# A kernel whose instruction order is planned at build time: the plan is refined backwards from the end, and block sums of v move to 32-column groups

## Chip, cores, metric

One core of one Trainium2 chip runs the program. The metric is device microseconds of one execution. PE is the matrix engine (PEld its weight loads), DVE the vector engine, ACT the scalar engine, POOL GpSimd, SP the engine that issues most DMA transfers.

## What is computed

Banded attention with block summaries, then a gated feed-forward layer, then a three-way maximum layer; all in 32-bit floats.

```
q, k, v: [2, 8, 768, 64]                       # batch, heads, sequence, head width
k_sum = max over blocks of 32 keys             # 24 per head
v_sum = mean over blocks of 32 values          # 24 per head
scores = [q k^T within |i-j| < 16,  q k_sum^T + log 32] / 8
x  = softmax(scores) @ [v, v_sum]              # -> [1536, 512]
x1 = (sigmoid(x w_gate) * (x w_val)) w_out     # 512 -> 1536 -> 512
h  = max(x1 w1, x1 w2, x1 w3)                  # 512 -> 768
out = h w_out2                                 # 768 -> 512
```

## The kernel before

The attention is cut into 16 units: a batch, a pair of heads p (4) and a half a of the sequence. Units 1 to 4 are batch 0, first half, head pairs 0 to 3; units 5 to 8 are its second half; units 9 to 16 are batch 1. A unit runs, in this order: scores on PE (L663), maximum with mask on DVE (`maxi`, L670, result `e`), exponential on ACT (`expo`, L676), reciprocal of the sum on DVE (L681, L682), scaling of one half on ACT (`scale`, L690) and, in the first eight units, of the other half on DVE (`norm`, L685), transposition on PE (`turn`, L695), copy to `at` on ACT (L701), product with v on PE (`pv`, L708), and the split of the result into two float parts `x`: the high part on ACT (L362), the low part on DVE (L365). Every operand of a large product is split so, and a product is three matmuls of 384 columns (a group of 6 or 12 in the listings is two or four such products).

The large products follow. L800 are the gate and value projections of batch 0, L839 the output projections, L1032 and L933 products of seven blocks in place of eight (a Strassen scheme) for batch 1 and for the second layer, L1133 the last layer. A projection of L800 needs `x` of head pair p for its quarter kc = p, so the quarter kc = 3 of the second half needs unit 8. L800 cannot start before the transpositions of units 1 to 4 (they use the same four PSUM banks, tag `m`). Weights arrive as 64-bit integers and are rebuilt by three DVE operations (L421, L426, L430), then split by ACT (L362, `w`) and DVE (L365).

Nothing of this order is written out by hand. `add(engine, duration, due, function, deps, new, uses, after)` makes a task; `Plan.order()` lists tasks forwards: at each step it takes, of the tasks that can start first on each engine, the one with the lowest due time, with durations and latencies that stand in the code. The due times are set by formulas of constants at the top of the file (`T - 11`, `due[key] + 2.4`). The order that comes out is the order of the instructions on every engine, and an engine runs its instructions strictly in that order. Where `order()` sees PE idle before the first products it adds matmuls of zeros on a tile `idle` (L1195), so as to keep PE busy.

The mean of the values over blocks of 32 is a product with a constant matrix `avg`, 96 rows by 128 columns, of which only columns 96 to 119 are not zero: v lies with 4 partial rows per partition step, 8 values in the free dimension. For batch 0 `vsum` does 8 matmuls of 128 columns that accumulate in one PSUM tile; `vcopy` (ACT, L595) brings the result to `vs`, and `vfill` (DVE, L654) puts it beside v in `vt`.

Of the kernel before, what the change touches and what calls it, by code (L numbers as in the profile page):

```python
# [37 lines left out]
JOINT = 1  # L38
SWITCH = 6.0
PAD = 2.0  # L40
SLACK = {"PE": 0.05, "DVE": 0.12, "ACT": 0.1, "POOL": 0.0, "SP": 0.0}
OVER = 0.0
SLOW = 1.12
# [31 lines left out]
class Plan:  # L75
# [42 lines left out]
    def order(self):  # L118
        engs = ("PE", "DVE", "ACT", "POOL", "SP")
        free = dict.fromkeys(engs, 0.0)  # L120
        free["SP"] = 0.6
        dge = ring = 0.0
        clock = self.Clock()
        free["PE"] = 1.13
        tab = "E"
        taken = {}
        wait, then, ready = {}, {}, {e: [] for e in engs}
        for t in self.tasks:
            pre = t.deps + t.after
            wait[t] = len(pre)  # L130
            for d in pre:
                then.setdefault(d, []).append(t)
            if not pre:
                ready[t.eng].append(t)
        out = []

        def earliest(t):
            at = free[t.eng]
            for d in t.deps:
                more = t.pad if d.eng != t.eng else 0.0  # L140
                if d.dma and d.end > self.CALM:
                    more = max(more, self.LATE)
                at = max(at, d.end + self.lag(d, t) + more)
            for d in t.after:
                at = max(at, d.start)
            need = {}
            for b in t.new:
                k = need.get(b.tag, 0)
                need[b.tag] = k + 1
                used = taken.setdefault(b.tag, [])  # L150
                i = len(used) + k - b.n
                if i >= 0:
                    for d in used[i].users:
                        if d.end is None:
                            return None
                        at = max(at, d.end + (self.LATE if d.dma and d.end > self.CALM else 0.1 if d.eng != t.eng else 0.0))
            return at

        def pressing(x):
            return x[1].due + (SWITCH if x[1].tab and x[1].tab != tab else 0.0)  # L160

        while len(out) < len(self.tasks):
            best = None
            for e in engs:
                c = [(at, t) for at, t in ((earliest(t), t) for t in ready[e]) if at is not None]
                if not c:
                    continue
                first = min(at for at, _ in c)
                at, t = min((x for x in c if x[0] <= first + SLACK[e]), key=pressing)
                if best is None or at < best[0]:  # L170
                    best = at, t
            at, t = best
            ready[t.eng].remove(t)
            t.start = at
            t.end = at + t.dur
            if t.eng == "PE":
                if t.new and at < FIRST + 5.0:
                    width = min(384, t.new[0].shape[-1] * (t.new[0].shape[1] if len(t.new[0].shape) == 3 else 1))
                    now = free["PE"]
                    while True:  # L180
                        end = clock.run(now, width / 2400.0, 1.0, False)
                        if end > at + OVER:
                            break
                        now = clock.run(now, width / 2400.0, 1.0) + 0.001
                        t.idle += 1
                    at = t.start = max(at, now)
                t.end = clock.run(at, t.dur, t.rows)
            if t.dma:
                dge = max(dge, at) + t.dma
                ring = max(ring, dge + 0.65) + (t.dur * SLOW if t.eng == "SP" else 0.2)  # L190
                free[t.eng] = at + t.dur if t.eng != "SP" else dge + 0.025
                t.end = ring
            if t.tab and t.tab != tab:
                tab = t.tab
                t.end += self.TABLE
            if not t.dma:
                free[t.eng] = t.end
            for b in t.new:
                taken[b.tag].append(b)
            out.append(t)  # L200
            for d in then.get(t, ()):
                wait[d] -= 1
                if not wait[d]:
                    ready[d.eng].append(d)
        return out


@with_exitstack
def kernel(
# [51 lines left out]
    ident = constant("ident", [128, 128])  # L261
    masks = constant("masks", [128, 3, CW])
    avg = constant("avg", [96, 128])

    def build_consts():
        make_identity(nc, ident)

        nc.gpsimd.memset(avg, 0.0)
        a = avg[:, 96:CW]
        nc.gpsimd.memset(a, 1.0 / BLK)  # L270
        nc.gpsimd.affine_select(
            out=a, in_=a, pattern=[[-4, NB]], compare_op=ALU.is_ge, fill=0.0,
            base=0, channel_multiplier=1)
        nc.gpsimd.affine_select(
            out=a, in_=a, pattern=[[4, NB]], compare_op=ALU.is_ge, fill=0.0,
            base=3, channel_multiplier=-1)


        nc.gpsimd.memset(masks[:, :, 0:96], 0.0)
        nc.gpsimd.memset(masks[:, :, 96:CW], math.log(BLK) / SC)  # L280
        for par in range(2):
            m = masks[64 * par:64 * par + 64, :, 0:96]
            nc.gpsimd.affine_select(
                out=m, in_=m, pattern=[[0, 3], [1, 96]], compare_op=ALU.is_ge, fill=BIG,
                base=-1, channel_multiplier=-1)
            nc.gpsimd.affine_select(
                out=m, in_=m, pattern=[[0, 3], [-1, 96]], compare_op=ALU.is_ge, fill=BIG,
                base=2 * WIN - 1, channel_multiplier=1)
        nc.gpsimd.memset(masks[0:64, 0, 0:WIN], BIG)
        nc.gpsimd.memset(masks[64:128, 2, 96 - WIN:96], BIG)  # L290
# [276 lines left out]
    def make_sums(b, p, T):  # L567

        kt, lk = load_task("k", BANKS_K, [128, S + 2 * WIN], kn[b, p], 1.14, T - (KEYS if b else KEYS0))
        r, lr = load_task("vn", 2, [96, 2, 8 * D], vn[b, p], 1.092, T - (SUMS if b else SUMS0))  # L570
        ks = Buf(ap_, [128, NB], F32, "ks", 4)
        vs = Buf(ap_, [128, 2 * D], F32, "vs", 4)
        ps = psum_s([128, 2 * D])

        def kmax():
            nc.vector.tensor_reduce(
                out=ks.t, in_=kt.t[:, WIN:WIN + S].rearrange("p (n w) -> p n w", w=BLK), axis=AX.X, op=ALU.max)

        def vsum():

            for n in range(8):
                nc.tensor.matmul(
                    ps.t, lhsT=avg, rhs=r.t[:, :, D * n:D * n + D], start=(n == 0), stop=(n == 7))

        def vadd():
            for n in (4, 2, 1):
                nc.vector.tensor_tensor(
                    out=r.t[:, :, 0:n * D] if n > 1 else vr.t, in0=r.t[:, :, 0:n * D],
                    in1=r.t[:, :, n * D:2 * n * D], op=ALU.add)

        def vmean():
            nc.tensor.matmul(ps.t, lhsT=avg, rhs=vr.t, start=True, stop=True)

        def vcopy():
            nc.scalar.activation(out=vs.t, in_=ps.t, func=ACTF.Copy)  # L595

        k = add("DVE", 0.87, T - 13.5, kmax, [lk], [ks], [kt])
        if b == 0:
            v1, v2 = None, add("PE", 1.75, T - 5, vsum, [lr, built], [ps], [r])
        else:  # L600
            lr.after.append(pvs[UPB - 1])
            vr = Buf(ap_, [96, 2, D], F32, "vr", 1)
            v1 = add("DVE", 1.2, T - 8, vadd, [lr, built], [vr], [r])
            v2 = add("PE", 0.22, T - 5, vmean, [v1], [ps], [vr])
            v2.pad = PAD
        v3 = add("ACT", 0.2, T - 4.5, vcopy, [v2], [vs], [ps])
        kblock[b, p] = ks, k, kt, lk
        vblock[b, p] = vs, v3
        attention.extend([k, v2, v3] + ([v1] if b else []))

    def make_unit(u, i):
        b, p, a = u
# [570 lines left out]
    with tc.manual_schedule():  # L1183
        idle = const.tile([128, 384], BF16, name="idle")
        nc.vector.memset(idle, 0.0)
        for t in plan.order():
            for b in t.new:
                b.take()
            if t.idle:

                o = t.new[0].t
                o = o if len(o.shape) == 2 else o.rearrange("p a c -> p (a c)")
                n = min(o.shape[1], 384)
                for _ in range(t.idle):
                    nc.tensor.matmul(o[:, 0:n], lhsT=idle[:, 0:128], rhs=idle[:, 0:n], start=True, stop=True)  # L1195
            t.fn()
# [59 lines left out]
```

## Time and profile before

| | |
|---|---|
| median of 3 executions | 545.08 us (544.48 to 546.09) |
| the profiled execution | 543.21 us |
| its span, first to last instruction | 541.3 us |
| PE busy | 532.0 us, 98% of the span |
| DVE, ACT, POOL busy | 419.7, 302.6, 3.7 us |
| mean granted PE clock | 0.996 of 2.4 GHz |

The 1.9 us by which the profiled execution is longer than its span lie outside of all instructions. PE's busy time contains the zero matmuls and time in which a matmul is only held in the pipeline, so that 98% does not say that the rest of 2% is all that could go. What PE does before the first L800 is a stage of its own; from there on its work is a fixed list.

### The profile page before, as it was taken

Reading aid. Unit: us, or ns where it says so; the run is one execution under the profiler, and the core shown is the slowest. Engines: PE = TensorE matmul, PEld = TensorE weight load, DVE = VectorE, ACT = ScalarE, POOL = GpSimd, SP = SyncE. Lnnn points to the kernel's source line nnn. Section 1 sums busy time; section 2 is a strip of 40 time slices with the busy share of each in tenths; the row PEclk is TensorE's granted clock in tenths of the full one; section 3 lists DMA queues with packets and bytes.
Section 4 is the critical chain, followed back from the end, with each engine's and each line's share of the span. In section 5 each row is a group of like instructions: output and inputs, shape, how many; then the busy total and the mean of one; then the engine's idle time right before and its main releaser. Section 6 shows DMA issues by size and latency. Waiting matters only on the chain.

```text
span 541.3 us, 10070 instructions
## 1 busy us (share of the span) xinstructions
PE 532.0 (98%) x3815; PEld 506.8 (94%) x3815; DVE 419.7 (78%) x988; ACT 302.6 (56%) x720; POOL 3.7 (1%) x18
## 2 busy tenths in 40 slices
PE   8999999999999999999999999999999999999997
PEld 6788898999999999999999999998999999998886
DVE  5999997899968358975487489999999998995000
ACT  5879876778656784664555167344334334363111
POOL 2000000000000000000000000000000000000000
PEclk9899999999999999999999999999999999999999
DMA  8999879989736010251252027102222232201121
GB/s 278 318 350 334 271 289 316 337 289 390 222 105 234 12 40 2 79 194 40 62 167 84 22 97 270 48 33 77 79 77 79 79 94 100 78 1 41 58 79 58
DMA packets 28128, 78.25 MB, mean 145 GB/s; under 512 B 3504, under 2 KB 6960, under 8 KB 28080
## 3 DMA queue, kind: packets, MB, share of 16 engines
q1 hardware_dynamic: 24960, 73.87, 40.2%
q10 hardware_dynamic: 3120, 3.74, 2.0%
q8 instruction: 30, 0.49, 0.4%
q14 instruction: 18, 0.15, 0.1%
HBM read 61.28 MB, written 15.73 MB: 142 GB/s over the span
## 4 chain that ended last, share of the span: by engine, by line
PE 78%; DVE 8%; ACT 6%; DMA 6%; issue 1%; SPq 0%; ACTq 0%; DVEq 0%
PE m L839 14%; PE m L800 13%; PE m L933 11%; PE s L933 11%; PE m L1133 9%; PE m L1032 8%; PE s L1032 8%; DMA k<-in_kn_dram 2%; PE s L708 2%; ACT e L690 1%; ACT e L676 1%; PE s L663 1%; DMA kept_o<-w 1%; DVE u L880 1%; DMA kept_v<-c 1%; PE s L695 1%
## 5 line engine op out<-in xcount | busy, mean ns | idle before, releaser
L800 PE MATMUL m<-x,w 128*128 128x384 f32 x576 | 108.9, 341 | 0.0
L839 PE MATMUL m<-h,w 128*128 128x384 f32 x576 | 105.5, 337 | 0.0
L800 PEld LDWEIGHTS m<-x,w 128*128 128x128 f32 x576 | 98.8, 188 | 2.2 <-issue 1.0
L839 PEld LDWEIGHTS m<-h,w 128*128 128x128 f32 x576 | 99.6, 188 | 0.5 <-issue 0.3
L933 PE MATMUL s<-f,w 128*128 128x384 f32 x294 | 56.1, 334 | 0.2 <-ACT tc L948 0.2
L933 PE MATMUL m<-x,w 128*128 128x384 f32 x294 | 56.1, 334 | 0.0
L933 PEld LDWEIGHTS s<-f,w 128*128 128x128 f32 x294 | 51.4, 188 | 0.5 <-ACT tc L948 0.5
L933 PEld LDWEIGHTS m<-x,w 128*128 128x128 f32 x294 | 51.5, 188 | 0.1
L1032 PE MATMUL s<-f,w 128*128 128x384 f32 x252 | 48.1, 335 | 0.1
L1032 PE MATMUL m<-f,w 128*128 128x384 f32 x252 | 46.9, 335 | 0.0
L1032 PEld LDWEIGHTS s<-f,w 128*128 128x128 f32 x252 | 43.9, 188 | 0.7 <-ACT t L1047 0.7
L1032 PEld LDWEIGHTS m<-f,w 128*128 128x128 f32 x252 | 43.9, 188 | 0.3 <-ACT tc L1047 0.2
L362 ACT ACTIVATE w<-c 128x512 fp32r<-128x512 f32 (+1 forms) x50 | 29.2, 588 | 22.5 <-DVE c L430 17.2
L676 ACT ACTIVATE e<-e,nm 128x120 f32<-128x120 f32 x96 | 36.7, 384 | 9.1 <-DVE nm L670 8.9
L365 DVE TENSOR_TENSOR w<-raw,w 128x512 fp32r<-128x512 f32 (+1 forms) x48 | 28.1, 618 | 15.9 <-ACT w L362 15.9
L362 ACT ACTIVATE h<-t 128x384 fp32r<-128x384 f32 x48 | 25.0, 522 | 20.0 <-DVE t L1072 12.2
L426 DVE SCALAR_TENSOR_TENSOR c<-raw,c 128x512 int32<-128x512 int32 x50 | 34.1, 683 | 0.4
L430 DVE SCALAR_TENSOR_TENSOR c<-raw,c 128x512 int32<-128x512 int32 x50 | 34.1, 681 | 0.3
L362 ACT ACTIVATE w<-raw 128x512 fp32r<-128x512 f32 (+1 forms) x48 | 25.6, 571 | 15.3 <-PE m L839 11.1
L365 DVE TENSOR_TENSOR w<-c,w 128x512 fp32r<-128x512 f32 (+1 forms) x50 | 31.7, 635 | 2.5 <-ACT w L362 2.3
L365 DVE TENSOR_TENSOR h<-t,h 128x384 fp32r<-128x384 f32 x48 | 26.2, 552 | 5.9 <-ACT h L362 5.4
L1143 ACT ACTIVATE c<-m 128x512 f32<-128x512 f32 (+1 forms) x13 | 7.3, 565 | 38.7 <-PE m L1133 38.2
(133 smaller groups left out, 805.8 us busy)
## 6 DMA issues: line engine op xcount, KB each, us to landing
raw<-in_wts_dram SPq DMA_DIRECT2D x60, 512.0 KB, 4.2
kept_o<-w SPq DMA_DIRECT2D x12, 512.0 KB, 4.1
w<-kept_o SPq DMA_DIRECT2D x12, 512.0 KB, 6.3
k<-in_kn_dram SPq DMA_DIRECT2D x8, 400.0 KB, 5.4
q<-in_qt_dram SPq DMA_DIRECT2D x16, 192.0 KB, 5.5
v<-in_vw_dram SPq DMA_DIRECT2D x16, 192.0 KB, 6.6
raw<-kept_g SPq DMA_DIRECT2D x6, 512.0 KB, 3.2
raw<-kept_v SPq DMA_DIRECT2D x6, 512.0 KB, 3.3
```

The costliest lines, as they stand in the source:

```text
L362: nc.scalar.activation(out=dst, in_=src, func=ACTF.Copy)
L365: nc.vector.tensor_tensor(out=dst, in0=src, in1=h.bitcast(F32), op=ALU.subtract)
L426: nc.vector.scalar_tensor_tensor(out=c.t, in0=half(r, 1), scalar=-0x40000000, in1=c.t, op0=ALU.bitwise_and, op1=ALU.bitwise_or)
L430: nc.vector.scalar_tensor_tensor(out=c.t, in0=half(r, 0), scalar=29, in1=c.t, op0=ALU.logical_shift_right, op1=ALU.bitwise_or)
L676: nc.scalar.activation(out=e[h].t[:, t], in_=e[h].t[:, t], func=ACTF.Exp, scale=-1.0, bias=nm.t[:, h, t:t + 1], accum_out=sm.t[:, h, t:t + 1])
L708: nc.tensor.matmul(px.t[64 * h:64 * h + 64, c:c + 64], lhsT=vt.t[:, t, par, h], rhs=at[h].t[0:CW, t, 64 * par:64 * par + 64], start=True, ...
L800: nc.tensor.matmul(ps.t, lhsT=w.t.rearrange("p s (k f) -> p s k f", k=KC)[:, wh, kc], rhs=src[kc // 2].t[:, xh, kc % 2], start=(kc == 0 an ...
L839: nc.tensor.matmul(ps.t, lhsT=w.t.rearrange("p s (k f) -> p s k f", k=KC)[:, wh, dm], rhs=h.t[:, xh], start=(i == 0 and j == 0), stop=(i = ...
L933: nc.tensor.matmul(ps.t, lhsT=w.t[:, wh, c:c + 128], rhs=x.t[:, xh, kc], start=new and n == 0, stop=n == 5, skip_group_check=True)
L1032: nc.tensor.matmul(ps.t, lhsT=w.t[:, wh, c:c + 128], rhs=x.t[:, xh, kc], start=new and n == 0, stop=n == 5, skip_group_check=True)
L1133: nc.tensor.matmul(ps.t[:, c0:c1], lhsT=h.t[:, xh, e, c:c + 128], rhs=w.t[:, wh, c0:c1], start=(f == 0 and i == 0), stop=(f == NF2 - 1 and ...
L1143: nc.scalar.activation(out=o.t[:, c0:c1], in_=ps.t[:, c0:c1], func=ACTF.Copy)
```

## The change

Three edits. `refined(2)` takes the place of `order()`: it runs `order()`, then `latest()`, which lists the same tasks backwards from the end of that plan and gives each the latest time at which it may begin; these become the due times of the next `order()`. Of the three orders the one with the earliest planned end is kept. In `order()` itself a transfer issued by ACT is now planned to end 3 us after its start. Third, the block sums of batch 0: each of the 8 matmuls takes only the columns 96 to 127 of `avg` and writes one of four groups of 32 partitions in PSUM, so that each group holds a quarter of the sum; ACT copies the four quarters to SBUF (`vkeep`, a new tile `vq`), and a further matmul with a new constant `fold` adds them (`vfold`). `fold` is built by four POOL copies ahead of `avg` and `masks`.

```diff
+REFINE = 2
...
-                t.end = ring
+                t.end = ring if t.eng == "SP" else at + 3.0
...
+    def latest(self, out):
...
+        for t in self.tasks:
+            for d in t.deps:
+                link(d, t, -(self.lag(d, t) + (t.pad if d.eng != t.eng else 0.0)))
+            for d in t.after:
+                link(d, t, d.dur)
...
+        end = max(t.end for t in out)
...
+        while ready:
+            t = max(ready, key=lambda t: (ready[t] if t.dma else min(ready[t], free.get(t.eng, end)), t.end))
+            at = ready.pop(t)
...
+                start[t] = free[t.eng] = min(at, free.get(t.eng, end)) - t.dur
...
+    def refined(self, times):
+        best = None
+        for i in range(times + 1):
+            out = self.order()
...
+            end = max(t.end for t in out)
+            if best is None or end < best[0]:
+                best = end, out, {t: t.idle for t in out}
+            start = self.latest(out) if i < times else None
+            for t in self.tasks:
+                if start:
+                    t.due = start[t]
...
+    fold = constant("fold", [128, 32])
...
+        for c in range(4):
+            nc.gpsimd.tensor_copy(fold[32 * c:32 * c + 32], ident[32 * c:32 * c + 32, 32 * c:32 * c + 32])
...
             for n in range(8):
+                c = 32 * (n % 4)
                 nc.tensor.matmul(
-                    ps.t, lhsT=avg, rhs=r.t[:, :, D * n:D * n + D], start=(n == 0), stop=(n == 7))
+                    ps.t[c:c + 32], lhsT=avg[:, 96:128], rhs=r.t[:, :, D * n:D * n + D], start=(n < 4), stop=(n >= 4),
+                    skip_group_check=True)
+
+        def vkeep():
+            nc.scalar.activation(out=vq.t, in_=ps.t, func=ACTF.Copy)
+
+        def vfold():
+            nc.tensor.matmul(ps.t[96:128], lhsT=fold, rhs=vq.t, start=True, stop=True)
...
-            v1, v2 = None, add("PE", 1.75, T - 5, vsum, [lr, built], [ps], [r])
+            vq = Buf(ap_, [128, 2 * D], F32, "vr", 1)
+            v1 = add("PE", 0.55, T - 7, vsum, [lr, built], [ps], [r])
+            v1 = add("ACT", 0.26, T - 6, vkeep, [v1], [vq], [ps])
+            v2 = add("PE", 0.24, T - 5, vfold, [v1], [], [vq, ps])
...
-        for t in plan.order():
+        for t in plan.refined(REFINE):
```

In the rows of order below, a number after a tile's name tells buffers apart, and xN counts instructions. The first place is PE where the first projection (L800 before, L884 in the change) stands; e_409 and e_410 before, e_445 and e_446 in the change, are the two halves of unit 4. Before:

```order
L582 MATMUL s<-vn,avg 128x128 x8
L663 MATMUL s<-k,q 64x96 x12
L663 MATMUL s<-ks,q 64x24 x12
L582 MATMUL s<-vn,avg 128x128 x8
L708 MATMUL s<-at,v 64x64 x12
L695 MATMUL m<-ident,e_409 120x128 x3
L695 MATMUL m<-ident,e_410 120x128 x3
L800 MATMUL m<-x,w 128x384 x6
```

The same place in the change:

```order
L792 MATMUL s<-at,v 64x64 x12
L1279 LDWEIGHTS idle
L1279 MATMUL s<-idle 128x128
...
L656 MATMUL s<-vn,avg 32x128 x8
L779 MATMUL m<-ident,e_445 120x128 x3
L779 MATMUL m<-ident,e_446 120x128 x3
L664 MATMUL s<-vr,fold 32x128
L884 MATMUL m<-x,w 128x384 x9
L747 MATMUL s<-k,q 64x96 x12
```

The product with v of unit 3 (L708, L792) moved ahead of the last block sum, and a fold now stands between unit 4's transpositions and the first projection. Ahead of it stand 4 scores, 4 pairs of transpositions, 3 products with v and 4 block sums in both.

The second place is ACT at unit 8, whose halves are e_929 and e_930 before, e_953 and e_954 in the change; the last row is the high part of its `x`. Before:

```order
L690 ACTIVATE e_929<-e_929,sm 128x120 x3
L817 ACT_TABLE_LOAD
L817 ACTIVATE t<-m 128x384
L701 ACTIVATE at<-s 120x384 x2
L362 ACTIVATE h<-t 128x384
L362 ACTIVATE w<-cx 128x512
L362 ACTIVATE w<-c 128x512
L362 ACTIVATE x<-s 128x384
```

In the change, where e_1097 is a half of unit 9:

```order
L785 ACTIVATE at<-s 120x384 x2
L901 ACTIVATE t<-m 128x384
L435 ACTIVATE h<-t 128x384 x2
L435 ACTIVATE w<-cx 128x512
L435 ACTIVATE h<-t 128x384
L760 ACT_TABLE_LOAD
L760 ACTIVATE e_1097,sm<-e_1097,nm 128x120 x3
L435 ACTIVATE x<-s 128x384
```

Between `at` and `x` of unit 8 stood three operations; now eight operations and a table load do, three of them exponentials of batch 1.

The third place is ACT in the first products of the second layer; `t<-m` are copies that PE's products wait for, `x<-u` and `x<-x` splits of 768 columns. Before:

```order
L362 ACTIVATE x<-u 128x768 x2
L1007 ACTIVATE h<-s 128x384
L948 ACTIVATE t<-m 128x384
L362 ACTIVATE x<-u 128x768 x2
L362 ACTIVATE x<-x 128x768
L948 ACTIVATE t<-m 128x384
L948 ACTIVATE tc<-s 128x384
```

In the change:

```order
L1091 ACTIVATE h<-s 128x384
L1032 ACTIVATE t<-m 128x384
L435 ACTIVATE x<-u 128x768 x2
L1032 ACTIVATE t<-m 128x384
L435 ACTIVATE x<-x 128x768
L1032 ACTIVATE tc<-s 128x384
```

The copy `t<-m` has moved ahead of the split `x<-x`.

## Rows read from the trace of the kernel before

**Rows 1.** The page: busy time, share of the span and instructions of each engine.
```profile
PE 532.0 (98%) x3815; PEld 506.8 (94%) x3815; DVE 419.7 (78%) x988; ACT 302.6 (56%) x720; POOL 3.7 (1%) x18
```

**Rows 2.** Windows: stretch, length, busy of PE PEld DVE ACT POOL, clock, DMA share, GB/s.
```profile
6.10:26.60 20.50, 18.54 (x334) 16.47 (x335) 18.84 (x78) 17.84 (x73) 0.00 (x0) 0.92 1.03 326
...
29.50:47.50 18.00, 17.44 (x220) 14.88 (x218) 17.68 (x61) 15.45 (x47) 0.00 (x0) 1.00 1.03 375
47.50:62.20 14.70, 14.68 (x167) 13.50 (x166) 14.47 (x45) 14.61 (x42) 0.00 (x0) 1.00 0.81 263
62.20:100.00 37.80, 37.29 (x308) 34.87 (x308) 32.12 (x87) 27.29 (x73) 0.00 (x0) 1.00 0.91 308
...
330.00:375.00 45.00, 43.62 (x248) 42.35 (x247) 44.65 (x77) 23.57 (x41) 0.00 (x0) 1.00 0.18 66
```

**Rows 3.** Timeline of PE at the first projection: start, length, line, tiles, xrecords.
```profile
26.06 2.05 PE L582 MATMUL s<-vn,avg 96*128 96x128 f32 x16
...
28.89 0.87 PE L695 MATMUL m<-ident,e 128*120 128x128 f32 x6
29.52 0.77 PE L800 MATMUL m<-x,w 128*128 128x384 f32 x3
```

**Rows 4.** Timeline of ACT there: the scaling of unit 4.
```profile
25.74 0.96 ACT L690 ACTIVATE e<-e,sm 128x120 f32<-128x120 f32 x3
```

**Rows 5.** ACT's groups in 6.1 to 26.6 us: busy, mean ns, idle before.
```profile
L676 ACT ACTIVATE e<-e,nm 128x120 f32<-128x120 f32 x24 | 9.1, 383 | 4.2 <-DVE nm L670 4.2
...
L701 ACT ACTIVATE at<-m 120x384 f32<-120x384 f32 x6 | 2.9, 485 | 1.4 <-PE m L695 1.4
L362 ACT ACTIVATE w<-c 128x512 fp32r<-128x512 f32 x2 | 1.2, 617 | 0.0
L362 ACT ACTIVATE x<-s 128x384 fp32r<-128x384 f32 x2 | 1.0, 478 | 0.0
L595 ACT ACTIVATE vs<-s 128x128 f32<-128x128 f32 x3 | 0.8, 263 | 0.4 <-PE s L582 0.4
```

**Rows 6.** Timeline of POOL and DVE: the last constant, the first maximum.
```profile
4.74 0.11 POOL L290 MEMSET masks<- 64x16 f32 x1
...
5.80 0.28 DVE L670 CUSTOM_DVE_ANT_0 e<-s,masks 128x120 f32<-128x120 f32 x1 [0.80 <-PE s L663]
```

**Rows 7.** Timeline of PE in the first 10 us: scores of unit 1, a block sum.
```profile
4.61 0.73 PE L663 MATMUL s<-k,q 64*64 64x96 f32 x24
...
6.77 2.02 PE L582 MATMUL s<-vn,avg 96*128 96x128 f32 x16 [0.68 <-DMA vn<-in_vn_dram]
```

**Rows 8.** Waits of PE from 29.5 to 375 us: total, times, longest.
```profile
PE m L933 <- ACT t L948: 1.1, 1, 1.1
PE s L695 <- ACT e L690: 0.7, 2, 0.5
```

**Rows 9.** Timeline of ACT ahead of PE's longest late wait.
```profile
369.01 0.83 ACT L362 ACTIVATE x<-x 128x768 fp32r<-128x768 f32 x1
369.75 0.47 ACT L948 ACTIVATE t<-m 128x384 f32<-128x384 f32 x1
```

**Rows 10.** Timeline of ACT at unit 8.
```profile
59.61 1.28 ACT L817 ACT_TABLE_LOAD   x1
...
61.29 0.87 ACT L701 ACTIVATE at<-s 120x384 f32<-120x384 f32 x2
...
63.49 0.50 ACT L362 ACTIVATE x<-s 128x384 fp32r<-128x384 f32 x1
```

**Rows 11.** Timeline of PE at unit 8.
```profile
62.17 0.96 PE L708 MATMUL s<-at,v 120*64 120x64 f32 x24
63.05 4.04 PE L800 MATMUL m<-x,w 128*128 128x384 f32 x21
```

**Rows 12.** Windows, columns as in rows 2: around the stretch of low clock.
```profile
14.87:18.28 3.41, 3.41 (x33) 2.92 (x34) 3.28 (x15) 2.94 (x12) 0.00 (x0) 0.50 1.04 348
10.00:14.87 4.87, 3.58 (x72) 3.34 (x71) 4.74 (x22) 4.15 (x19) 0.00 (x0) 1.00 1.03 358
```

More of the change, by code (lines that the diff above doesn't have):

```diff
@@ L205, in order, with link, until @@
         return out
+    def latest(self, out):
+        then, before = {}, {}
+        def link(a, b, room):
+            then.setdefault(a, []).append((b, room))
+            before.setdefault(b, []).append(a)
+        for t in self.tasks:
[3 more added lines that the diff above has]
+                link(d, t, d.dur)
+        taken = {}
+        for t in out:
+            for b in t.new:
+                used = taken.setdefault(b.tag, [])
+                used.append(b)
+                if len(used) > b.n:
+                    for d in used[-1 - b.n].users:
+                        link(d, t, -0.1 if d.eng != t.eng else 0.0)
+        end = max(t.end for t in out)
+        free = {}
+        start, left = {}, {t: len(then.get(t, ())) for t in self.tasks}
+        ready = {}
+        def until(t):
+            return min([end] + [start[s] + room for s, room in then.get(t, ())])
+        for t in self.tasks:
+            if not left[t]:
+                ready[t] = until(t)
+        while ready:
+            t = max(ready, key=lambda t: (ready[t] if t.dma else min(ready[t], free.get(t.eng, end)), t.end))
+            at = ready.pop(t)
+            if t.dma and t.eng == "SP":
+                free["SP"] = min(at, free.get("SP", end)) - t.dur * SLOW
+                start[t] = free["SP"] - 2.0
+            elif t.dma:
+                start[t] = at - (t.end - t.start)
+            else:
+                start[t] = free[t.eng] = min(at, free.get(t.eng, end)) - t.dur
+            for d in before.get(t, ()):
+                left[d] -= 1
+                if not left[d]:
+                    ready[d] = until(d)
+        return start
@@ new lines, in refined @@
+    def refined(self, times):
+        best = None
+        for i in range(times + 1):
+            out = self.order()
+            if out is None:
+                break
+            end = max(t.end for t in out)
+            if best is None or end < best[0]:
+                best = end, out, {t: t.idle for t in out}
+            start = self.latest(out) if i < times else None
+            for t in self.tasks:
+                if start:
+                    t.due = start[t]
+                    t.start = t.end = None
+                    t.idle = 0
+        for t, n in best[2].items():
+            t.idle = n
+        return best[1]
@@ L587, in vadd @@
                 nc.vector.tensor_tensor(
-                    out=r.t[:, :, 0:n * D] if n > 1 else vr.t, in0=r.t[:, :, 0:n * D],
+                    out=r.t[:, :, 0:n * D] if n > 1 else vr.t[0:96].rearrange("p (h d) -> p h d", h=2), in0=r.t[:, :, 0:n * D],
                     in1=r.t[:, :, n * D:2 * n * D], op=ALU.add)
         def vmean():
-            nc.tensor.matmul(ps.t, lhsT=avg, rhs=vr.t, start=True, stop=True)
+            nc.tensor.matmul(ps.t, lhsT=avg, rhs=vr.t[0:96], start=True, stop=True)
         def vcopy():
-            nc.scalar.activation(out=vs.t, in_=ps.t, func=ACTF.Copy)
+            nc.scalar.activation(out=vs.t[96:128], in_=ps.t[96:128], func=ACTF.Copy)
         k = add("DVE", 0.87, T - 13.5, kmax, [lk], [ks], [kt])
         if b == 0:
-            v1, v2 = None, add("PE", 1.75, T - 5, vsum, [lr, built], [ps], [r])
+            vq = Buf(ap_, [128, 2 * D], F32, "vr", 1)
+            v1 = add("PE", 0.55, T - 7, vsum, [lr, built], [ps], [r])
+            v1 = add("ACT", 0.26, T - 6, vkeep, [v1], [vq], [ps])
+            v2 = add("PE", 0.24, T - 5, vfold, [v1], [], [vq, ps])
         else:
             lr.after.append(pvs[UPB - 1])
-            vr = Buf(ap_, [96, 2, D], F32, "vr", 1)
+            vr = Buf(ap_, [128, 2 * D], F32, "vr", 1)
             v1 = add("DVE", 1.2, T - 8, vadd, [lr, built], [vr], [r])
@@ L608, in make_sums @@
         vblock[b, p] = vs, v3
-        attention.extend([k, v2, v3] + ([v1] if b else []))
+        attention.extend([k, v2, v3, v1])
     def make_unit(u, i):
```

## The prediction

> **What bounds the kernel now.** I read the page first. PE is busy for 98% of the span [rows 1], so only what PE does before its fixed list of large products, and the gaps in that list, can go. That calls for a table by stage, with the projection's start (29.52 us) as the border [rows 3]. From there on PE's work is the same list of products before and after: by the order, 4 scores, 4 pairs of transpositions, 3 products with v and 4 block sums stand ahead of the first projection in both kernels. So the end moves by what the first projection moves, plus what PE's gaps behind it change.
>
> The gaps behind it are small [rows 2]: 18.00 - 17.44 = 0.56 us up to 47.5, 0.02 up to 62.2, 0.51 up to 100, and 45.00 - 43.62 = 1.38 from 330 to 375, 2.5 us in all. The waits say what ended them: a scaled `e` that a transposition waits for, and one copy by ACT of 1.1 us [rows 8]. So what is left to win lies mostly ahead of 29.52.
>
> There, ACT and DVE carry the time. From 6.1 us, where the exponentials begin, to 26.6, where unit 4 has been scaled, ACT is busy for 17.84 of 20.50 us and DVE for 18.84 [rows 2]; both run a chain through four units. ACT's idle time is 2.66 us, of which 1.4 + 0.4 us ended with PE's transpositions and block sums [rows 5]; the exponentials' 4.2 us there are mostly the wait for the first maximum, before 6.1. Then PE takes over: unit 4 is scaled at 25.74 + 0.96 = 26.70 [rows 4], but PE stands in a block sum from 26.06 to 28.04, then does unit 3's product with v, and only then, at 28.89, unit 4's transpositions [rows 3]. The reader is to see that PE, full of gaps filled with zero products elsewhere in this stage, is on the path in its last 2.8 us.
>
> **The block sum.** Eight matmuls, 16 records, take 2.02 us [rows 7]. Four column groups at a time are not in the trace; bounds: 2.02 us if they still run one after another, a quarter of it, 0.5, if four overlap. The scores, whose matmuls use quarters of the array, are the nearest row: 24 records of 96 columns within 0.73 us, where at the block sum's 2.02 / 16 = 0.126 us for 128 columns they would take 24 x 0.095 = 2.3 [rows 7]. So overlap is real, and I take 0.6. In the new order the last block sum stands ahead of the transpositions behind zero products, its operands long there, so that even 2 us would be over while ACT still scales unit 4.
>
> The Trainium skill, page "TensorEngine Tiling (Array Packing)", section "Tiling Modes", speaks for and against: 128x32 tiles run four at a time, but a change of tiling mode drains the engine, and each block sum now enters and leaves a mode. The trace shows overlap in the scores; of the drain no row here has a price by itself. By the fourfold figure alone the sum takes 0.5 us, an estimate, and the forecast stays.
>
> **What the sums add.** ACT copies the four quarters: 0.26 us each, as for the copy of the same shape [rows 5]. The fold is one matmul of 128 columns, two records: 0.25 us by the block sum's rate. POOL builds `fold` ahead of the masks, the last of which is set at 4.85 us while the first maximum starts at 5.80 [rows 6]; four small copies, at 0.1 to 0.3 us each as POOL's last row, end the masks at 5.25 to 6.05, so they cost 0 to 0.3; I take 0.1.
>
> **The start of the projections.** Up to unit 4's scaling the new order holds on ACT the same operations as before but for three copies of quarters (3 x 0.263) and one split `x` (0.478) more and one split `w` (0.617) less [rows 5]: +0.65 us. DVE has 0.7 us less there. The idle 2.66 us: at the most all of it goes, at the least none. The part that PE caused, 1.8 us, is what shorter sums and the new places of the transpositions can take; waits between DVE and ACT stay. I take half of 2.66, 1.33. So unit 4 is scaled at 26.70 + 0.65 + 0.1 - 1.33 = 26.1. Then, in place of 29.52 - 26.70 = 2.8 us, come the transpositions (0.63 from 28.89 to 29.52 [rows 3]) beside ACT's split (0.62) and copy (0.26), and the fold (0.25) that stands ahead of the first projection: 1.13. The first projection starts at 27.25, **2.3 us earlier**. Bounds: no idle time gone and 0.3 for POOL gives 28.8 (0.7 earlier); all of it gone gives 25.8 (3.7).
>
> **The gaps behind.** At 369 us PE waits for a copy that stands on ACT behind a split of 369.75 - 369.01 = 0.74 us [rows 9]; the new order has the copy first: -0.7. Of the 0.56 and 0.51 us at transpositions I take half, since the units are ordered anew and nothing tells which wait goes: -0.5. Together **-1.2**, between 0 and -2.5.
>
> **What is late next.** Unit 8. Before, its `x` starts at 63.49, 1.3 us after its `at` ends at 62.16 [rows 10]. Now three exponentials of unit 9 and a table load stand between. A copy and four splits take 2.5 us by their row means, 0.48 and once 0.62 [rows 5], less 0.09 each by which ACT's rows overlap (0.83 against 0.74 [rows 9]), so 2.1; the table load 1.28 [rows 10]; three exponentials 3 x 0.383 = 1.15 [rows 5]: 4.5 us. With `x` high and low (about 0.9) unit 8 is ready 5.4 us after its `at`. PE can meanwhile do the product with v (0.9) and at most 21 more products: 111 stand ahead of it, 96 of them the first half, and four PSUM banks hold three quarters (9 products) each, 96 + 36 = 132; 21 took 4.0 us [rows 11]. So PE waits up to 0.5 us, or 1.5 if a bank is late: **+0.5**. DVE is nearly full from 29.5 to 62.2 (17.68 of 18.00, 14.47 of 14.70 [rows 2]); this is the tightest part.
>
> **Sum:** -2.3 - 1.2 + 0.5 = -3.0. The profiled execution took 543.2 us and would take 540.2. It lies 1.9 us under the median of the runs shown, and the same difference against that median, 545.08, gives **542.1 us**.
>
> **The rivals.** A measurement of this kernel can tell about 0.3%, 1.6 us, from no change: faster is below 543.4, slower above 546.7.
>
> *Everything goes.* All of ACT's idle time (3.7 earlier), all gaps (-2.5), nothing at unit 8: -6.2, 538.9. For it speaks that an order with due times from the end serves what the end needs; against it the DVE waits among ACT's.
>
> *Paid back.* The start is earlier, but units 5 to 8 are no earlier, since DVE and ACT have almost no free time up to 62.2 (ACT 14.61 of 14.70 in the last part [rows 2]), and PE waits for them. Only the late copy is left: -0.7, 544.4. Against it: ACT was idle for 18.00 - 15.45 = 2.55 us up to 47.5, and by the order its work up to unit 8's `at` is the same to 0.1 us.
>
> *Low clock.* From 14.87 to 18.28 us PE ran at half of 2.4 GHz, after a stretch in which it was busy for 3.58 of 4.87 us [rows 12]. The sums now give PE 4 x 1.4 us less to do, filled with a little more of zero products. If such a stretch of 3.41 us falls behind the first projection, PE loses half of it, 1.7: -3.0 + 1.7 = -1.3, 543.8. The Trainium skill, page "TensorE: Matmul & The Clock Gate", Part 1, says that idle time takes the clock to half rate, and the trace agrees, with clock 0.50.
>
> *Slower.* Due times that are the latest possible leave no lead: before, constants asked for weights 8 us ahead. If each of the 48 gated results `h` that the output projections read came late by 0.15 us on a PE that has no gap there now, that were 7 us against the 3.5 won: +3.7, 548.8. It decides once the waits between 62 and 330 us pass 5 us. Against it: the listing still runs forwards, and an engine that is free takes a task however late its due time is; DVE is free for 5.7 of 37.8 us from 62.2 on [rows 2].
>
> That the change does nothing to the order is excluded: the first piece of order shows it changed.
>
> **How the numbers follow.** The forecast with its own range, 540.3 to 543.4 (start 1.4 to 3.3 earlier, gaps as above), gets 0.50; everything goes 0.17; paid back 0.17; low clock 0.06; slower 0.10. Paid back and low clock count as the same but for a quarter of them, which falls below 543.4. So faster 0.73, same 0.17, slower 0.10. The range that holds 8 in 10 goes from 539.2 to 545.4: it leaves out the slower case and the far ends of "everything goes" and of "paid back".
>
> **What would show it.** Right: the first projection at 26.5 to 28 us, the block sum within 0.5 to 0.8 us, unit 4's transpositions within 0.5 us after its scaling, no wait of 1 us for the copy near 366 us. Wrong: the block sum still at 2 us; the first projection at 28.8 or later; a wait of PE over 1.5 us for unit 8 between 58 and 66 us; waits of PE on `h` or `w` that pass 2 us between 62 and 330; a low clock behind 27 us.

## The result

The changed kernel took 539.64 us (median of 4 runs, 539.13 to 540.56) against 544.89 us, a ratio of 0.988 (95% interval 0.986 to 0.991; the two medians by themselves give 0.990). Run again it took 540.60 us (6 runs, 539.55 to 542.52) against 545.10: 0.992 (0.990 to 0.995). It is 4.5 to 5.3 us faster; 3.0 us were forecast. The time lies in the range, close to its lower end, but the gain is half as large again or more, and it does not lie where the forecast put it.

**The profile after.** The profiled execution took 539.13 us, span 537.4 (before 543.21 and 541.3). First the page and the windows, to lay beside [rows 1, 2]:

```profile
PE 528.9 (98%) x3850; PEld 503.8 (94%) x3850; DVE 419.1 (78%) x988; ACT 303.5 (56%) x724; POOL 4.5 (1%) x22
...
6.10:26.60 20.50, 18.02 (x396) 13.93 (x389) 18.10 (x79) 17.83 (x73) 0.00 (x0) 0.92 0.99 314
...
29.50:47.50 18.00, 18.00 (x289) 16.50 (x288) 17.70 (x64) 17.10 (x57) 0.00 (x0) 1.00 1.03 358
47.50:62.20 14.70, 14.25 (x147) 12.21 (x147) 14.57 (x51) 14.61 (x38) 0.00 (x0) 1.00 0.89 312
62.20:100.00 37.80, 37.00 (x270) 35.86 (x266) 32.33 (x78) 28.31 (x73) 0.00 (x0) 1.00 0.91 300
...
330.00:375.00 45.00, 44.81 (x258) 44.19 (x257) 44.68 (x79) 22.92 (x41) 0.00 (x0) 1.00 0.18 59
```

PE's idle time from 330 to 375 us fell from 1.38 to 0.19 us. ACT's from 6.1 to 26.6 is 2.67 us, as before (2.66), where half of it was to go. The next to last column, the share of the DMA engines, was 1.03 and is 0.99 there: the transfers fill that stage in both kernels.

PE's and ACT's timelines at the first projection [rows 3, 4], and PE's first scores and block sum [rows 7]:

```profile
26.12 1.18 PE L1279 MATMUL s<-idle 128*128 128x128 bf16 x18
27.23 0.65 PE L656 MATMUL s<-vn,avg 96*32 96x128 f32 x16
27.80 0.87 PE L779 MATMUL m<-ident,e 128*120 128x128 f32 x6
28.60 0.41 PE L664 MATMUL s<-vr,fold 128*32 128x128 f32 x2
28.94 0.96 PE L884 MATMUL m<-x,w 128*128 128x384 f32 x4
...
26.66 0.97 ACT L774 ACTIVATE e<-e,sm 128x120 f32<-128x120 f32 x3
...
4.61 1.24 PE L747 MATMUL s<-k,q 64*64 64x96 f32 x24
...
6.62 0.64 PE L656 MATMUL s<-vn,avg 96*32 96x128 f32 x16
```

The block sum takes 0.64 us for 2.02. Unit 4's transpositions stand right behind its scaling (27.63 to 27.80), and the first projection follows 1.31 us after the scaling instead of 2.82. But the scaling itself ends 0.93 us later than before, so the projection starts at 28.94 us, 0.58 earlier.

ACT's groups in that stage [rows 5], GpSimd's and VectorE's rows [rows 6], and what PE waits for in the whole program (total, times, longest), of which the two rows of [rows 8] are gone:

```profile
L760 ACT ACTIVATE e<-e,nm 128x120 f32<-128x120 f32 x24 | 9.1, 384 | 4.7 <-DVE nm L754 4.7
...
L785 ACT ACTIVATE at<-m 120x384 f32<-120x384 f32 x6 | 2.7, 489 | 0.6 <-PE m L779 0.6
...
L676 ACT ACTIVATE vs<-s 32x128 f32<-32x128 f32 x3 | 0.8, 270 | 0.8 <-PE s L664 0.8
...
1.45 0.95 POOL L339 COPY fold<-ident 32x32 f32<-32x32 f32 x4
...
5.86 0.11 POOL L363 MEMSET masks<- 64x16 f32 x1
...
6.41 0.28 DVE L754 CUSTOM_DVE_ANT_0 e<-s,masks 128x120 f32<-128x120 f32 x1 [1.57 <-PE s L747]
...
PE s L656 <- DMA vn<-in_vn_dram: 1.0, 1, 1.0
PE m L884 <- ACT t L901: 0.8, 1, 0.8
PE s L747 <- issue: 0.7, 1, 0.7
PE s L747 <- DMA q<-in_qt_dram: 0.7, 1, 0.7
```

The idle time that PE's transpositions caused on ACT fell (1.4 to 0.6), and other waits took its place: 0.5 us more for the first maximum (6.41 for 5.80 us), 0.8 at the fold, and on PE 1.7 us for transfers of `vn` and `q`. The first maximum stood waiting for PE's scores of unit 1, which took 1.24 us in this execution (0.73 before), and not for the masks, which end at 5.97 us. That is no work of the change: in two more profiles of the kernel before (b_again2, b_again3 below) these scores also take 1.24 us, and the maximum starts at 6.57 and 6.45 us.

The late copy [rows 9] now stands ahead of the split; and at unit 8 [rows 10, 11] ACT's copy `t` (L901), whose bank PE needs, stands behind three scalings of unit 9 and a table load:

```profile
366.18 0.47 ACT L1032 ACTIVATE t<-m 128x384 f32<-128x384 f32 x1
366.54 0.84 ACT L435 ACTIVATE x<-x 128x768 fp32r<-128x768 f32 x1
...
66.64 0.97 ACT L774 ACTIVATE e<-e,sm 128x120 f32<-128x120 f32 x3 [0.20 <-DVE sm L766]
67.63 1.28 ACT L901 ACT_TABLE_LOAD   x1
68.93 0.49 ACT L901 ACTIVATE t<-m 128x384 f32<-128x384 f32 x1
...
69.47 2.72 PE L884 MATMUL m<-x,w 128*128 128x384 f32 x14 [0.80 <-ACT t L901]
```

### The profile page after: what moved, and what is told of

The parts are those of the page before. It is cut to its first block, busy times and chain, and to the rows that moved or that the text cites. A ratio compares the mean times of both kernels' runs of the same rounds, so it can differ in the third digit from the quotient of the medians.

```text
span 537.4 us, 10140 instructions
## 1 busy us (share of the span) xinstructions
PE 528.9 (98%) x3850; PEld 503.8 (94%) x3850; DVE 419.1 (78%) x988; ACT 303.5 (56%) x724; POOL 4.5 (1%) x22
## 4 chain that ended last, share of the span: by engine, by line
PE 87%; DVE 7%; DMA 2%; ACT 1%; issue 1%; SPq 1%; ACTq 0%
PE m L923 19%; PE m L884 14%; PE s L1017 12%; PE m L1017 12%; PE m L1217 9%; PE m L1116 8%; PE s L1116 8%; PE s L792 2%; DMA vn<-in_vn_dram 1%; PE s L747 1%; PE s L779 1%; DMA raw<-in_wts_dram 1%; DVE c L503 1%; DVE e L754 1%; SPq L630 1%
## 5 line engine op out<-in xcount | busy, mean ns | idle before, releaser
L884 PE MATMUL m<-x,w 128*128 128x384 f32 x576 | 108.6, 340 | 1.0 <-ACT t L901 0.8
L884 PEld LDWEIGHTS m<-x,w 128*128 128x128 f32 x576 | 98.7, 188 | 3.5 <-ACT t L901 1.3
L1032 ACT ACTIVATE tc<-s 128x384 f32<-128x384 f32 x27 | 13.3, 491 | 27.8 <-PE s L1017 27.7
```

Of the source, the lines that this page charges most:

```text
L884: nc.tensor.matmul(ps.t, lhsT=w.t.rearrange("p s (k f) -> p s k f", k=KC)[:, wh, kc], rhs=src[kc // 2].t[:, xh, kc % 2], start=(kc == 0 an ...
L1032: return t, after(tag, add("ACT", 0.37, end(k), lambda: nc.scalar.activation(out=t.t, in_=ps.t, func=ACTF.Copy), [p], [t], [ps]))
```

## The experiments

Two theories stood against each other at first. A, as predicted: the start of the first projection carries the gain. B: the late stage and the gaps behind the start carry it, by the order. The second group of runs added D: ahead of the projections the transfers set the pace. Each run of the first group has one profile, and the start of the first projection differs by 3 us between executions of one kernel (table below), so a start and a "rest of the span" given for such a run are those of one execution.

**e1_sums** (`REFINE = 2` becomes `REFINE = 0`)

> The new block sums alone: work is listed forwards once, by the old due times. Theory A (as predicted: the start of the first projection carries the gain, and sums and order both serve it): the sums free PE of 4 x 1.4 us ahead of it, the first projection starts 0.5 to 1.5 us before 29.5 us, the copy of 1.1 us near 366 us still holds PE up, and the time is 0.5 to 1.5 us under that of before. Theory B (the second layer's start carries it, by the order alone): the first projection moves by no more than the 0.6 us of the changed kernel, PE's large products around 353 to 370 us win nothing, time 0 to 0.6 us under before. Theory C (the sums alone are the change): 4 to 5 us under before.

The edit leaves in the new planning of transfers that ACT issues (`at + 3.0`), so the run has that edit and the sums together. Measured 543.77 us, ratio 0.997 (0.996 to 0.999). PE's wait of 1.1 us for the late copy is there, and 1.2 us by the medians is A's size; B's "0 to 0.6" fails. But A's place does not hold: the first projection starts at 29.94 us (with one more unit's scores ahead of it), and the gain of this execution, one of the fastest of its kernel (541.90 us), lies behind it, where the rest of the span is 510.2 us for 511.8.

**e2_refine**

```diff
+REFINE = 2
-                t.end = ring
+                t.end = ring if t.eng == "SP" else at + 3.0
+    def latest(self, out):
...
-        for t in plan.order():
+        for t in plan.refined(REFINE):
```

> The refined order alone, with the old block sums of 128 columns (2.02 us each). Theory A: without the shorter sums the first projection starts at 28.5 to 29.5 us, the late copy no longer holds PE up: 1 to 2 us under before. Theory B: the second layer's start gives its 2.1 us and the stretch up to 100 us its 1.0 as in the changed kernel, only the 0.6 us of the start are lost: 3 to 4 us under before. Theory C: no change, within 0.5 us of before.

Measured 541.15 us, ratio 0.994 (0.992 to 0.996): 3.8 us by the medians, B's size. Its profile, of an execution of 543.47 us, starts the projection as late as 34.02 us, and the rest of the span is 507.6 us. PE's granted clock was 0.50 there from 19.9 to 30.1 us, so this start says little of the order. By the medians the order is worth more than what e1_sums has (3.8 for 1.2 us), and by this profile behind the start. The planning of ACT's transfers is in both runs; no run has it alone, and what it is worth is not shown.

**e3_late**

```diff
+        for t in self.tasks:
+            t.due = best[2][t] if chosen(first[t]) else first[t]
...
+        for t in plan.refined(REFINE, lambda d: d >= due["P", "a", 0, 0, 1] - 25.0):
```

> New sums; refined due times only for the tasks due from 25 us ahead of the second layer's first large product on, the old due times for all earlier ones. Theory A: what the late order is worth was put at 0.7 us, beside 0.5 to 1.5 for the sums: 1.2 to 2.2 us under before. Theory B: by the changed kernel's trace the stretch from 353 to 370 us gains 2.1 us, and so here, from whatever point the products reach there: the time of the sums alone less 2.1 us, or 2 to 2.7 us under before.

Measured 541.68 us, ratio 0.993 (0.991 to 0.996): 2.1 us under e1_sums, B's figure.

**e4_early** (the complement, `d < due[...] - 25.0`)

> New sums; refined due times only for the tasks due before 25 us ahead of the second layer's first large product, the old ones behind. PE's and SP's order is the same as in the changed kernel, ACT's and VectorE's differ only in the late stage. Theory A: all but the late 0.7 us stays: 0.7 us above the changed kernel. Theory B: the late stage's 2.1 us are lost, so 2 us above the changed kernel and about 2 to 3 us under before, with the first projection where the changed kernel has it, at 28.9 us, and a wait of PE of 0.7 to 2 us near 366 us.

Measured 541.70 us, ratio 0.994 (0.991 to 0.996), 1 to 2 us above the changed kernel; PE's late wait is back:

```profile
PE m L1020 <- ACT t L1035: 1.1, 1, 1.1
```

So e1_sums (0.3%), the early order (0.4%) and the late order (0.4%) add up to about the whole; each of these ratios is uncertain by about 0.2%.

**a_again**

> The changed kernel once more, for a narrower interval and a second profiled execution. If its four times of 539.1 to 540.6 us are typical, the ratio is 0.988 to 0.991 and the first projection starts again near 28.9 us. Theory D (the stage ahead of the projections is paced by transfers, whose rate differs between executions; the DMA share is 0.98 to 1.02 from 2 to 40 us): the start of the first projection differs between the two profiled executions by 0.5 us or more, with the waits of PE on vn and q, and everything behind 100 us repeats within 0.3 us.

Measured as above, 540.60 us, ratio 0.992. The first projection started at 29.38 us, 0.44 us later than in the first profile, a little less than D asked for. PE waited 3.1 us for `vn`, and the span less the start was 508.42 us, against 508.46 in the first profile: all of the difference between the two lies ahead of the start.

**e5_fold_last** (the four copies for `fold` moved behind the last mask)

> The changed kernel with GpSimd's four copies for the fold matrix behind the masks. Theory A (the chain of maximum, exponential and scaling sets the start): the first maximum starts at 5.8 us in place of 6.4, and the first projection and the end come 0.3 to 0.6 us earlier. Theory D (transfers set it): the first maximum starts earlier, but the later waits on vn and q grow by as much, and the time stays within 0.3 us.

Measured 540.17 us (540.01 to 540.44), ratio 0.991 (0.989 to 0.993); against 540.60 that is not told apart from nothing. The start in its profile is 30.06 us. Neither theory's first maximum came: with the last mask set at 4.86 us it starts at 6.58, behind scores of unit 1 that again take 1.24 us. So GpSimd's copies did not hold it up, and this run says nothing on what an earlier maximum would be worth.

**e7_half_vn** (block means of half the rows)

```diff
+                if tag == "vn" and first:
+                    nc.sync.dma_start(out=b.t[r0:r1, :, 0:4 * D], in_=src[r0:r1, :, 0:4 * D])
...
-                    ps.t[c:c + 32], lhsT=avg[:, 96:128], rhs=r.t[:, :, D * n:D * n + D], start=(n < 4), stop=(n >= 4),
+                    ps.t[c:c + 32], lhsT=avg[:, 96:128], rhs=r.t[:, :, D * (n % 4):D * (n % 4) + D], start=(n < 4), stop=(n >= 4),
```

> The changed kernel, but the block sums of the first half load only half of vn (192 of 384 KB, four times) and sum that half twice, so the block means are those of half the rows; no instruction of PE, VectorE or ACT moves. 0.77 MB less is transferred by 20 us, 2.5 us at the 310 GB/s of that stage. Theory A (the chain of the engines sets the start): only PE's wait of 1.0 us for vn shrinks, the end comes 0 to 0.6 us earlier. Theory D (transfers set it): the first projection starts 1 to 2.5 us earlier, ACT's idle time between 6.1 and 26.6 us falls by 1 us or more, and the end comes 1 to 2.5 us earlier.

Measured 538.06 us (537.45 to 538.71), 2.5 us under the changed kernel beside it; its slowest run is under every run of the changed kernel. The first projection starts at 27.68 us, and ACT's idle time in the stage falls from 2.63 to 1.58 us. Windows of a_again and then of this kernel, columns as in [rows 2]:

```profile
6.10:26.60 20.50, 16.11 (x381) 12.40 (x379) 17.85 (x79) 17.87 (x73) 0.00 (x0) 1.00 0.98 303
```
```profile
6.10:26.60 20.50, 18.30 (x423) 14.15 (x419) 19.12 (x81) 18.92 (x77) 0.00 (x0) 1.00 0.95 310
```

With no instruction of an engine moved, fewer bytes alone make DVE and ACT busier there. That is D: A allowed 0.6 us.

**e8_rate** (`SLOW = 1.12` becomes `SLOW = 1.2`)

> The changed kernel, but the order is made for transfers that take 1.2 times their nominal time in place of 1.12 (400 KB in 1.37 us, 299 GB/s; the changed kernel's trace shows 304 to 338 GB/s up to 40 us). Theory D: with the sums' loads ahead of the weights, PE's waits on vn and q in the first 20 us go, and the end comes 0.5 to 1 us earlier, with less spread. Theory A: within 0.5 us of the changed kernel, either way.

Measured 540.60 us, ratio 0.992 (0.990 to 0.994), the same as the changed kernel. Its profile starts the projection at 28.19 us, but the rest is 509.71 us: the wait for `t` grew to 1.9 us in two places. What the loads won ahead was given back behind, and D's 0.5 to 1 us did not come.

**b_again, b_again2** (the kernel before)

> The kernel before once more, for a second profiled execution. Theory D (the spread of its times, 543.3 to 547.3 us, is that of the transfers ahead of the projections): the span less the start of the first projection is again 511.8 us within 0.2, and what the time differs by from 543.2 us is found in that start. Rival (the spread lies in the whole program, as in the copies behind 330 us): the start stays at 29.5 us and the difference is found behind it.

> As the run ahead of it: a third profiled execution of the kernel before. Theory D: span less start 511.8 us within 0.2; the rival: start 29.5 us.

Measured 545.91 and 546.76 us, and neither theory's picture: the starts are 28.82 and 31.68 us, and the rest is 515.18 and 513.22, not 511.8. The old order loses in both parts. Where it loses behind the start is seen in b_again, in VectorE's, ACT's and PE's timelines:

```profile
88.73 0.43 DVE L421 TENSOR_SCALAR c<-raw 128x512 int32<-128x512 int32 x1 [2.01 <-DMA kept_g<-c]
...
92.28 0.43 DVE L421 TENSOR_SCALAR c<-raw 128x512 int32<-128x512 int32 x1 [0.57 <-DMA kept_v<-c]
92.74 0.69 DVE L426 SCALAR_TENSOR_TENSOR c<-raw,c 128x512 int32<-128x512 int32 x1
93.47 0.69 DVE L430 SCALAR_TENSOR_TENSOR c<-raw,c 128x512 int32<-128x512 int32 x1
...
94.27 0.19 DVE L682 RECIPROCAL sm<-sm 128x6 f32<-128x6 f32 x1
...
94.56 1.25 ACT L690 ACTIVATE e<-e,sm 128x120 f32<-128x120 f32 x4 [1.13 <-DVE sm L682]
...
95.01 0.90 PE L695 MATMUL s<-ident,e 128*120 128x128 f32 x3 [1.14 <-ACT e L690]
...
120.62 0.92 PE L708 MATMUL s<-at,v 120*64 120x64 f32 x24 [1.60 <-DMA v<-vs]
```

VectorE waits until a transfer has stored an earlier weight tile, converts the next one, and only then computes the reciprocal for which ACT's scaling and PE's transposition stand waiting. By this chain PE's wait is 0.51 us in the first profile [rows 8], 1.14 and 0.97 in these; and once a product with v waits 1.60 us for a transfer at 120 us, one of those that ACT issues. The changed kernel's profiles have neither wait.

**e9_swap, e10_both**

```diff
+        i = next(i for i, t in enumerate(todo) if t.tab == "S" and t.start > 64.0)
+        j = max(j for j in range(i) if todo[j].eng == "ACT")
+        todo.insert(i, todo.pop(j))
```

> The changed kernel with one move on ACT: the table load and the copy (sigmoid) of unit 8's quarter that PE waits for at 69.5 us stand ahead of three scalings of unit 9, which take 0.97 us. If that one place is what unit 8 being late costs, PE's wait of 0.8 us there shrinks to 0 to 0.2, the span less the start of the first projection falls from 508.4 to 507.5 to 507.9 us, and the time by 0.5 to 0.9 us. Rival: the scalings, 1.8 us later, make PE wait at unit 9's transpositions, and nothing is won.

> That move on ACT together with GpSimd's copies behind the masks. By theory D the copies matter little (0 to 0.3 us), by the move the span less the start falls to 507.5 to 507.9 us: 0.5 to 1.2 us under the changed kernel, 0.6 at the likeliest.

Measured 539.22 us, ratio 0.991 (0.989 to 0.993), and 539.62 us, ratio 0.992 (0.990 to 0.995), against 540.60 for the changed kernel in other runs: the lowest medians with the full computation but not told apart from it by time. By the profile the move does what it should: the wait for `t` is gone, and the rest is 507.57 and 507.45 us in place of 508.42.

**b_half_vn, a_again2, a_again3, b_again3** (the first again means of half the rows, by the edit of e7_half_vn)

> The kernel before with half of vn loaded in the first half (192 of 384 KB, four times, that half summed twice: the block means are those of half the rows), nothing else moved. Its three profiled executions differ in the start of the first projection (28.82 to 31.68 us) and in the rest (511.8 to 515.2), where PE waits for a scaled tile at 94 to 97 us (0.51 to 1.14) and once 1.60 for a transfer at 120. Theory D (late transfers cause both): the start falls to 26.5 to 28.5 us, the rest stays at 511.8 or below it, and the median falls by 2.5 us or more. Theory A (the chain of the engines): the start stays within 0.6 us of 29, the time within 0.6 us.

> The changed kernel, a third profiled execution: whether its start differs from that of before in the mean. Theory A says 2.3 us earlier than before, whose mean of three is 30.0 us: 27.7. What the traces of the changed kernel show so far, 28.94 and 29.38, says 28.9 to 30.1, with the span less the start at 508.4 us.

> A fourth profiled execution of the changed kernel: start of the first projection 28.9 to 30.1 us, the rest 508.4 us within 0.1, as in the run ahead of it.

> A fourth profiled execution of the kernel before: start 28.8 to 31.7 us, the rest 511.8 to 515.2 us. If the rest is again above 512, the changed order wins by what transfers that come late cost the old one behind the start.

b_half_vn took 543.76 us against 546.08, ratio 0.996 (0.993 to 0.998). Its start, 28.48 us, is earlier than all of the old kernel's, but its rest is 514.22 us, and PE's wait at the transposition of 95 us is 1.46 us, the longest of all. D's claim that fewer bytes would also shorten the rest failed: the stores that VectorE waits for do not come earlier because the start does. Its wait for `kept_g`, 2.01 us in the rows above, is 2.55 us here. The others took 542.17, 540.61 and 545.88 us. From PE's timelines and the spans, in us ("rest" is the span less the start; it is split after the first 864 matmuls of the large products):

| profile | start of first projection | rest |
|---|---|---|
| before | 29.52 | 511.78 = 187.3 + 324.5 |
| b_again | 28.82 | 515.18 = 190.7 + 324.5 |
| b_again2 | 31.68 | 513.22 = 188.7 + 324.6 |
| b_again3 | 30.60 | 513.40 = 188.8 + 324.6 |
| after | 28.94 | 508.46 = 186.3 + 322.2 |
| a_again | 29.38 | 508.42 = 186.3 + 322.2 |
| a_again2 | 31.98 | 508.42 = 186.3 + 322.2 |
| a_again3 | 29.61 | 509.18 = 187.1 + 322.1 |

The means are 30.16 and 29.98 for the start, 513.40 and 508.62 for the rest: 0.2 and 4.8 us, 5.0 together, which is what the medians show. With 3 us between executions, four profiles of each leave the difference of the starts uncertain by about 2 us. But four more profiles have this order of PE ahead of the start (e4_early, e5_fold_last, e9_swap, e10_both: 29.51, 30.06, 30.43 and 30.15 us), and none of the eight comes near the 27.25 us that was forecast.

## Why the prediction was wrong

**The step that failed is the start of the first projection, "2.3 us earlier".** It moved by 0.58 us in the profiled pair and by 0.2 in the means of four, with 3 us between executions of one kernel. Its parts on PE were right: the block sum 0.64 us (0.6 forecast), the transpositions 0.17 us behind the scaling, 1.31 us from there to the projection (1.13). The term that was wrong is "I take half of 2.66": none of ACT's idle time went, since transfers set the pace of that stage. The DMA share of 1.03 stood in [rows 2], and the prediction read only the busy columns beside it. e7_half_vn shows the cause: with 0.77 MB less the projection starts 1.3 to 4.3 us ahead of the four starts, and 1.05 us of ACT's idle time goes; what holds the other 1.58 us is not shown. GpSimd's copies take 0.95 us and the masks end at 5.97, near the far end of the bounds, yet the 0.1 us taken for them holds: in a_again3, where unit 1's scores take 0.82 us, the first maximum waits for the masks and starts at 5.91 us (5.80 before), and in e5_fold_last it was no earlier without the copies. The step ahead of it, that PE's work in front of the first projection is the same before and after, holds, though PE's timelines show five scores there and not four, in both kernels.

**The gaps behind, "-1.2", were mis-sized.** Behind the first 864 matmuls 2.4 us went (by the means, 324.54 to 322.15) where 0.7 stood. The row of 1.1 us [rows 8] is not the price of the stall. In PE's timeline of before

```profile
367.95 1.21 PE L933 MATMUL s<-x,w 128*128 128x384 f32 x6
370.27 1.31 PE L933 MATMUL m<-f,w 128*128 128x384 f32 x6 [1.12 <-ACT t L948]
```

six matmuls that follow each other at 0.173 us begin at 367.95, so the seventh was due at 368.99 and came at 370.27: 1.28 us. From the second layer's first large product on, the next 344 matmuls took 61.80 us before and 59.88 after, so 1.9 of the 2.4 us lie there; a second stall there, at 357 us, whose wait reads 0.21, costs 0.37 by the same count (six matmuls from 356.00, the next at 357.41). e1_sums (61.83), e4_early (61.35) and e3_late (60.23) show that it comes and goes with the late order on ACT.

**In the first 864 matmuls from the start on** the forecast was 0 (-0.5 at transpositions, +0.5 for unit 8); it was -1.0 in the profiled pair and -2.4 in the means. The wait for the scaled `e` near 94 us went altogether, which was priced by half of the 0.51 us that one execution showed; in the others it is about 1. Unit 8 costs 0.85 us by e9_swap, not 0.5, and for a bank held by ACT's copy, which the prediction had only as its upper bound.

So for -2.3, 0 and -0.7 us the means of four show -0.2, -2.4 and -2.4. That the time still fell into the range is luck: two us were missing ahead of the start, and four more than forecast went behind it.

**The rivals.** "Slower" needed waits on `h` and `w` of 5 us: there are 0.2. "Low clock" did not come behind the start. "Everything goes" (538.9) came nearer in time, but it put 3.7 of its 6.2 us ahead of the start. "Paid back" described the old order better than the new: with b_half_vn and b_again the old one started early and lost it near 95 us, while the changed one kept all of e7_half_vn's gain (rest 508.43).

**The profiled execution** of before was at the low end of its kernel's times (543.21; its runs reach from 542.84 to 550.52). Carrying its distance from the median, 1.9 us, over to the new kernel hid that the new order is also steadier behind the start: rest within 0.8 us over four profiles, for 3.4.

What stays open: which of the transfers ahead of the start is the slow one in a given execution; what the planning of ACT's transfers is worth, which no run has alone; and why e1_sums loses the wait at 94 us too. That planning is one candidate, since e1_sums has it, but the orders differ there in many places.

## What to carry to other kernels

Before costing a chain of engines, read the DMA share of the same window: where it is near 1.0, as here, do not count an engine's idle time as won by shortening another engine until a run with fewer bytes has shown what the transfers hold. Cost a stall of PE by the distance of the product starts around it, not by the wait's row. And take several profiles of the kernel before, with the start and the rest apart: what differs between them tells which stage the transfers pace and which waits of one profile are larger in others.

## What was not expected of the hardware

One stretch of half clock [rows 12] does not set the start: the granted clock from 6.1 to 26.6 us was 0.92 in the profile after, with a start of 28.94 us, and 1.00 in a_again with 29.38. Where it was 0.83, with 6.8 us at half clock (a_again2, e9_swap), the start was later, 31.98 and 30.43. In both PE was already waiting when the clock fell, in the middle of unit 3's scores. In a_again2:

```profile
17.31 0.42 PE L747 MATMUL s<-ks,q 64*64 64x24 f32 x7 [2.25 <-issue]
```

PE stood from 15.06 us on, and the clock fell at 16.9; in e9_swap it stood from 15.0 to 15.6, and the clock fell at 15.5. For this wait the profile names no releaser; it is 0.73 to 0.75 us in the other three profiles of the changed kernel. The two starts differ by 1.55 us and the two waits by 1.64, so the latest start of the changed kernel is that wait rather than the clock. As an estimate, the half clock itself cost at most 1 us: e9_swap started 0.4 to 1.0 us behind the three profiles at full clock with a like wait (a_again, a_again3, e5_fold_last: 29.38, 29.61, 30.06). In e2_refine, where half clock lasted up to the last block sum, one block sum took 3.28 us (2.00 at full clock), and the start was the latest of all.

16 matmul records of 32 columns in four column groups took 0.64 us, a third of 2.02. The Trainium skill, page "TensorEngine Tiling (Array Packing)", section "Tiling Modes", lists four 128x32 tiles that work independently of each other. The trace agrees: the records start in bunches of four, 0.11 to 0.13 us from one bunch to the next, and 0.11 us was the distance from one record to the next before. The 0.64 us end with the length of the last record, 0.27 us, which does not shrink; that is why the row is not a quarter of 2.02.
